# Linear attention ahead of a Mish feed-forward on one core: the side of each attention product that stands still on TensorE, how x is divided and turned, and where the key units run

## The chip, the cores and the metric

The program runs on one NeuronCore of a Trainium2 chip. The metric is the device time of one execution in microseconds (us), and for the kernel before it is the median of three runs. A run can also leave a profile, and its span is the time from the first to the last recorded instruction.

## What is computed

There are 8 batches, 8 heads, 576 tokens, head width 64 and 128 features. With x for q or k:

```python
proj = x @ w_phi                                  # 64 -> 128
proj = proj - max(abs(proj), axis=-1)
phi  = concat([exp(proj), exp(-proj)], axis=-1)   # 256 features
kv   = sum over tokens of phi(k)[f] * v[d]        # 256 x 64 for each batch and head
z    = sum over tokens of phi(k)[f]
x    = (phi(q) @ kv) / (phi(q) @ z + 1e-6)        # 4608 tokens x 512 after the heads are joined
h    = x @ w_in                                   # 512 -> 2048
out  = (h * tanh(softplus(h))) @ w_out            # 2048 -> 512 (this h*tanh(softplus) is Mish)
```

The weights of the feed-forward arrive as float64 words and are turned to float32 on the core.

## The kernel before, in words

**Number forms.** A float32 product is done in one of two ways. In plain float32 each matmul of the program becomes two instructions of TensorE. Or an operand is split into a high and a low part in the type float32r, and three products (high by high, high by low, low by high) are added up; each is one instruction. The feed-forward uses three products throughout.

**Feed-forward.** The 4608 tokens are 18 chunks of 256. For each chunk, 16 steps `ff_in` (L364) make h, twelve matmuls of 256 columns each; `mish` applies Mish on ScalarE two steps at a time and splits the result into `gh` and `gl`; 16 steps `ff_out` (L395) add up the output, six matmuls of 512 columns each. They follow each other with a lag of some four steps.

**Attention, keys.** A key unit is 256 tokens of a head pair (or the end of one pair and the beginning of the next): `k_load`, `k_proj` and `k_sum`. There are 72, nine to a batch. `project` (L161) multiplies keys by `w_phi` in six matmuls of 256 columns into `pp_k`; VectorE takes the largest absolute value (`m_k`, L146) and subtracts it (`d_k`, L165); ScalarE makes both exponentials. In `k_sum` (L223) the sums over tokens have **v as the stationary operand** (66 columns: 64 of v, one of ones for z, one of zeros) and both exponentials moving, 256 columns, in plain float32, into `kvps`. The result lies the wrong way round, so it is copied (`kvT`), turned by four transposes (`kvt`, L230), copied again, and written to DRAM, from which `kv_load` reads it back when queries need it.

**Attention, queries.** A query unit is one of four head pairs `cc` of a chunk `c`. `project_stacked` (L177) makes `pp_q` with four matmuls of 256 columns; `q_turn` (L262) turns the result by four transposes into `dt_q`; `q_exp` makes both exponentials and splits each into `eh` and `el`; `q_kv` splits `kv` into `kvs`. `q_num` (L313) has **kv as the stationary operand** (66 columns) and the exponentials moving: twelve matmuls where the chunk lies in one batch, 24 shorter ones where it touches two. Its result is already transposed for `ff_in`. The denominators are one row of it, so `q_den` sends them through DMA onto many partitions (`dp`), takes the reciprocal, writes it to DRAM (`r`) and spreads it back (`rb`); `q_out` multiplies on GpSimd and splits x into `xTh` and `xTl`. The first chunk's projection and sums are done in plain float32.

**What sets the order.** A list of events with due times, in units of one feed-forward step, gives the program order: all 72 key units and the first chunk's four query units come 1.1 units apart before step 0, the weight pieces (32 of 512 KB, each loaded and then converted by VectorE, ScalarE and GpSimd) are spread evenly over the same time, and the query units of chunk c+1 run at a pitch of four steps among the feed-forward of chunk c. A scheduler then orders each engine's queue; each engine works its queue strictly in order. All DMAs are issued by the SP queue. PSUM has four buffers `att` for all attention results, two for h and two for the output; before step 0, `project` uses the two of h and `kvps` the two of the output.

Of the kernel before, what the change touches and what calls it, by code (L numbers as in the profile page):

```python
# [27 lines left out]
NRAW, NE, NEH, NEL, NV, NKV = 3, 4, 2, 2, 2, 5  # L28
NHALF, NX, NRB, NXT, NG = 2, 2, 1, 3, 4

GP, GQ, GV = 2.2, 2.2, 1.5
GK, VLOAD = 2.7, 1.5
LOAD, WLOAD, KVLOAD = 4.0, 3.0, 3.0
Q0, Q1, QOUT, QL = -1.0, 4.0, 4.5, 0.5
QPOS, UPRE = 60, 1.1
W0, W1 = 4.0, 2.0
LAG, TAIL, TAILLAG = 4, 10, 2

KPLAIN, QPLAIN = 1, 1

NSPARE, WIN, MSPARE = 32, 4, 5
# [3 lines left out]
def attention_then_mish(ctx, tc, qT, kT, va, w_phi, w_in, w_out, out):  # L45
# [5 lines left out]
    dram = ctx.enter_context(tc.tile_pool(name="dram", bufs=4, space=bass.MemoryType.DRAM))  # L51
# [13 lines left out]
    def raw_tile(name):  # L65
        return work.tile([P, 2, 2 * P], F32, tag="raw", name=name, bufs=NRAW)

    def half_tile(name):
        return work.tile([P, 512], F32, tag="half", name=name, bufs=NHALF)


    wphi_raw = moe.tile([P, 2 * F], F32, tag="xTh", name="wphi_raw", bufs=NXT)
    nc.sync.dma_start(wphi_raw, w_phi[0])
    wphi_hi = moe.tile([P, 2 * F], F32R, tag="gh", name="wphi_hi", bufs=NG)
    wphi_lo = moe.tile([P, 2 * F], F32R, tag="gl", name="wphi_lo", bufs=NG)
    nc.vector.tensor_copy(wphi_hi, wphi_raw)
    nc.vector.tensor_sub(wphi_lo, wphi_raw, wphi_hi.bitcast(F32))
    wst_raw = moe.tile([P, 2 * F], F32, tag="xTl", name="wst_raw", bufs=NXT)
    nc.sync.dma_start(wst_raw, w_phi[1])
# [10 lines left out]
    spare = [f"w{kind}_{i}_{j}" for kind, i, j in pieces[-NSPARE:]]  # L90
    turn = 0
# [5 lines left out]
    def pair_tile(name):  # L97
        nonlocal turn
        if len(spare) >= MSPARE:
            turn += 1  # L100
            return slot_tile(spare[turn % min(WIN, len(spare))], F32, name)
        return work.tile([P, 2, 512], F32, tag="e", name=name, bufs=NE)

    piece = 0

    def load_weight(kind, i, j):
        nm = f"{kind}_{i}_{j}"
        if f"w{nm}" in spare:
            spare.remove(f"w{nm}")
        src = w_in[i * P:(i + 1) * P, j * 512:(j + 1) * 512] if kind == "in" else w_out[i * P:(i + 1) * P, :]  # L110
        slot = f"w{kind}_{i}_{j}"
        words = slot_tile(slot, U32, f"words_{nm}").rearrange("p a b -> p (a b)")
        nc.sync.dma_start(words, src.bitcast(U32))
        weight[kind, i, j] = words.rearrange("p (a b) -> p a b", b=2)

    def split_weight(kind, i, j):

        nonlocal piece
        nm = f"{kind}_{i}_{j}"
        slot = f"w{kind}_{i}_{j}"  # L120
        words = weight[kind, i, j]
        low, high = words[:, :, 0], words[:, :, 1]
        tag, bufs = ("u", 3) if piece % 5 < 3 else ("ee", 2)
        piece += 1
        w = moe.tile([P, 512], U32, tag=tag, name=f"w_{nm}", bufs=bufs)
# [10 lines left out]
        parts = slot_tile(slot, F32R, slot)  # L136
# [5 lines left out]
    def less_max(d, name):  # L142

        d3 = d.rearrange("p (n f) -> p n f", f=F)
        m = work.tile([P, 4], F32, tag="m", name=f"m_{name}", bufs=3)
        nc.vector.tensor_reduce(m, d3, axis=AX.X, op=ALU.max, apply_absolute_value=True)  # L146
        return d3, m.unsqueeze(2).broadcast_to([P, 4, F])

    def project(raw, plain, name):

        parts = ((raw, wphi_raw),)
        if not plain:
            hl = work.tile([P, 2, 2 * P], F32R, tag="hl", name=f"hl_{name}")
            hi, lo = hl[:, 0, :], hl[:, 1, :]
            nc.scalar.copy(hi, raw)  # L155
            nc.gpsimd.tensor_sub(lo, raw, hi.bitcast(F32))  # L156
            parts = ((hi, wphi_hi), (hi, wphi_lo), (lo, wphi_hi))
        ps = (ps_h if starting else ps_att).tile([P, 512], F32, tag="h" if starting else "att", name=f"pp_{name}")
        for i in range(2):
            for k, (x, w) in enumerate(parts):  # L160
                nc.tensor.matmul(ps[:, i * 2 * F:(i + 1) * 2 * F], x[:, i * P:(i + 1) * P], w,  # L161
                                 start=(k == 0), stop=(k == len(parts) - 1))
        d = pair_tile(f"d_{name}")
        p3, m = less_max(ps, name)
        nc.vector.tensor_tensor(d[:, 0, :].rearrange("p (n f) -> p n f", f=F), p3, m, op=ALU.subtract)  # L165
        return d

    def project_stacked(raw, name):

        x = work.tile([P, 2, 2 * P], F32R, tag="hl", name=f"hl_{name}")  # L170
        nc.scalar.copy(x, raw)  # L171
        nc.gpsimd.tensor_sub(x[D:], raw[D:], x[D:].bitcast(F32))  # L172
        d = pair_tile(f"d_{name}")
        for i in range(2):
            ps = ps_att.tile([P, 2, 2, F], F32, tag="att", name=f"pp{i}_{name}")
            for j in range(2):
                nc.tensor.matmul(ps[:, j], x[:, j, i * P:(i + 1) * P], wst, start=True, stop=True)  # L177
            di = d[:, 0, i * 2 * F:(i + 1) * 2 * F].rearrange("p (j f) -> p j f", f=F)
            nc.scalar.copy(di, ps[:, :, 1, :])
            nc.vector.tensor_tensor(di, ps[:, :, 0, :], di, op=ALU.add)  # L180
# [101 lines left out]
    def batches(c):  # L282
        return range(c * CH // S, (c * CH + CH - 1) // S + 1)
# [213 lines left out]
```

## Time and profile before

| what | value |
|---|---|
| median of three runs | 1228.69 us (1226.5 to 1229.23) |
| the profiled execution | 1229.93 us |
| its span | 1228.0 us |
| mean granted TensorE clock | 0.996 |
| busy in the span: PE / PEld / DVE / ACT / POOL | 1199.2 / 1064.4 / 597.2 / 895.2 / 594.9 us |
| instructions of PE and of PEld | 8094 each |

PE is TensorE's matrix products, PEld its loads of the stationary operand, DVE VectorE, ACT ScalarE, POOL GpSimd, SPq the queue that issues DMAs. A load can run while the product ahead of it streams, so PE and PEld overlap. The end of a matmul is modelled, so the time of one is best read from the distance between starts. In a group "128*66 128x256" the stationary operand has 128 partitions and 66 columns, and 256 columns move. A float32 matmul shows as two instructions.

### The profile page before, as it was taken

Reading aid. Unit: us, or ns where it says so; the run is one execution under the profiler, and the core shown is the slowest. Engines: PE = TensorE matmul, PEld = TensorE weight load, DVE = VectorE, ACT = ScalarE, POOL = GpSimd, SP = SyncE. Lnnn points to the kernel's source line nnn. Section 1 sums busy time; section 2 is a strip of 40 time slices with the busy share of each in tenths; the row PEclk is TensorE's granted clock in tenths of the full one; section 3 lists DMA queues with packets and bytes.
Section 4 is the critical chain, followed back from the end, with each engine's and each line's share of the span. In section 5 each row is a group of like instructions: output and inputs, shape, how many; then the busy total and the mean of one; then the engine's idle time right before and its main releaser. Section 6 shows DMA issues by size and latency. Waiting matters only on the chain.

```text
span 1228.0 us, 21711 instructions
## 1 busy us (share of the span) xinstructions
PE 1199.2 (98%) x8094; PEld 1064.4 (87%) x8094; DVE 597.2 (49%) x987; ACT 895.2 (73%) x1704; POOL 594.9 (48%) x509
## 2 busy tenths in 40 slices
PE   8999998899999999999999999999999999999998
PEld 6776776688999899999999999999999999999997
DVE  6987887954443344334443444334343444344211
ACT  6887877788777767777777777777777777777531
POOL 3765665856544545454444544545454544544200
PEclk9999999899999999999999999999999999999999
DMA  5665657311111211110121111111111111010000
GB/s 194 206 187 176 200 159 229 99 57 36 53 44 40 61 31 51 38 53 27 49 65 36 44 28 56 31 53 27 57 61 32 44 40 53 27 36 14 25 24 18
DMA packets 62025, 84.87 MB, mean 69 GB/s; under 512 B 17632, under 2 KB 35808, under 8 KB 61920
## 3 DMA queue, kind: packets, MB, share of 16 engines
q1 hardware_dynamic: 61920, 83.49, 22.0%
q8 instruction: 63, 1.03, 0.3%
q14 instruction: 42, 0.34, 0.1%
HBM read 69.40 MB, written 13.91 MB: 68 GB/s over the span
## 4 chain that ended last, share of the span: by engine, by line
PE 81%; DVE 7%; DMA 5%; ACT 2%; issue 2%; POOL 1%; SPq 0%; POOLq 0%; DVEq 0%
PE h L364 33%; PE o L395 32%; PE num_q L313 8%; PE kvps L223 3%; PE pp_q L177 2%; PE dt_q L262 2%; DMA words_out<-w_out 2%; DMA words_in<-w_in 2%; DVE m_k L146 1%; DVE d_k L165 1%; PE pp_k L161 1%; DVE scale_in L133 1%; DVE scale_out L128 1%; DMA rb<-r 1%; DVE w_in L132 1%
## 5 line engine op out<-in xcount | busy, mean ns | idle before, releaser
L364 PE MATMUL h<-xTh,win 128*128 128x256 f32 x2304 | 466.3, 284 | 0.0
L381 DVE TENSOR_TENSOR gl<-u,gh 128x256 fp32r<-128x256 f32 x288 | 169.1, 613 | 479.6 <-ACT gh L380 476.5
L364 PEld LDWEIGHTS h<-xTh,win 128*128 128x128 f32 x2304 | 378.2, 190 | 9.4
L395 PE MATMUL o<-wout,gh 128*128 128x512 f32 x1152 | 364.5, 396 | 0.0
L364 PE MATMUL h<-xTl,win 128*128 128x256 f32 x1152 | 325.3, 283 | 0.0
L279 POOL TENSOR_TENSOR el_q<-d_q,eh_q 128x512 fp32r<-128x512 f32 x136 | 180.0, 1335 | 295.4 <-ACT eh_q L278 295.4
L364 PEld LDWEIGHTS h<-xTl,win 128*128 128x128 f32 x1152 | 219.0, 190 | 6.8
L395 PE MATMUL o<-wout,gl 128*128 128x512 f32 x576 | 224.8, 391 | 0.0
L395 PEld LDWEIGHTS o<-wout,gh 128*128 128x128 f32 x1152 | 198.4, 189 | 25.8
L223 PE MATMUL kvps<-d_k,v 128*66 128x256 f32 x640 | 151.9, 383 | 5.4 <-ACT d_k L207 4.4
L172 POOL TENSOR_TENSOR hl_q<-qraw,hl_q 64x512 fp32r<-64x512 f32 x68 | 88.5, 1301 | 105.5 <-ACT hl_q L171 90.2
L272 ACT ACTIVATE d_q<-dt_q 128x512 f32<-128x512 f32 x144 | 86.1, 601 | 71.6 <-PE dt_q L262 71.3
L395 PEld LDWEIGHTS o<-wout,gl 128*128 128x128 f32 x576 | 108.3, 188 | 23.8
L223 PEld LDWEIGHTS kvps<-d_k,v 128*66 128x66 f32 x640 | 86.0, 139 | 48.2 <-ACT d_k L207 6.7
L380 ACT CAST gh<-u 128x256 fp32r<-128x256 f32 x288 | 109.0, 406 | 20.5 <-PE o L395 11.9
L372 ACT ACTIVATE u<-h 128x512 f32<-128x512 f32 x144 | 86.1, 598 | 49.7 <-PE h L364 49.0
L313 PE MATMUL num_q<-eh_q,kvs 128*66 128x256 f32 (+3 forms) x736 | 107.9, 255 | 0.9 <-ACT eh_q L278 0.9
L298 POOL TENSOR_TENSOR kvs<-kv,kvs 128x264 fp32r<-128x264 f32 x92 | 81.4, 895 | 19.3 <-ACT kvs L297 13.7
L313 PE MATMUL num_q<-el_q,kvs 128*66 128x256 f32 (+3 forms) x368 | 88.9, 256 | 1.2 <-POOL el_q L279 1.2
L372 ACT ACT_TABLE_LOAD x69 | 88.5, 1283 | 1.2
L156 POOL TENSOR_TENSOR hl_k<-kraw,hl_k 128x256 fp32r<-128x256 f32 x71 | 60.5, 856 | 57.8 <-ACT hl_k L155 57.7
L161 PE MATMUL pp_k<-wphi_hi,hl_k 128*128 128x256 f32 x284 | 76.3, 331 | 10.9 <-DVE d_k L165 9.8
(74 smaller groups left out, 1694.9 us busy)
## 6 DMA issues: line engine op xcount, KB each, us to landing
qraw<-qT SPq DMA_DIRECT2D x136, 128.0 KB, 3.0
v<-va SPq DMA_DIRECT2D x32, 330.0 KB, 3.4
kraw<-kT SPq DMA_DIRECT2D x36, 256.0 KB, 3.5
rb<-r SPq DMA_DIRECT2D x72, 128.0 KB, 3.0
out<-osb SPq DMA_DIRECT2D x36, 256.0 KB, 2.1
words_in<-w_in SPq DMA_DIRECT2D x16, 512.0 KB, 4.4
words_out<-w_out SPq DMA_DIRECT2D x16, 512.0 KB, 4.1
kvd<-kvo SPq DMA_DIRECT2D x32, 132.0 KB, 1.8
```

The costliest lines, as they stand in the source:

```text
L161: nc.tensor.matmul(ps[:, i * 2 * F:(i + 1) * 2 * F], x[:, i * P:(i + 1) * P], w, start=(k == 0), stop=(k == len(parts) - 1))
L172: nc.gpsimd.tensor_sub(x[D:], raw[D:], x[D:].bitcast(F32))
L223: nc.tensor.matmul(kv_ps[pair][:VW, j], vt[:, slot, j, :], e[:, :, (2 * i + j) * F:(2 * i + j + 1) * F], start=(slot == 0 and j == 0), sto ...
L272: nc.scalar.activation(e, ps, AF.Exp, scale=2.0 * s - 1.0)
L279: nc.gpsimd.tensor_sub(el, e, eh.bitcast(F32))
L298: nc.gpsimd.tensor_sub(wl, w, wh.bitcast(F32))
L313: nc.tensor.matmul(ps[:VW, j, r0:r1], w[:, j, s, :], e[:, j * CH + r0:j * CH + r1], start=first, stop=(s == 1 and k == len(parts) - 1), sk ...
L364: nc.tensor.matmul(ps, w[:, wcol], x[:, cc % 2, :], start=(n == 0), stop=(n == 11))
L372: nc.scalar.activation(u, hv, AF.Mish)
L380: nc.scalar.copy(gh, u[:, f * CH:(f + 1) * CH])
L381: nc.vector.tensor_sub(gl, u[:, f * CH:(f + 1) * CH], gh.bitcast(F32))
L395: nc.tensor.matmul(ps, g[:, cols], w, start=(i == 0 and k == 0), stop=(i == NFT - 1 and k == 2))
```

## The change

Every product of the attention now has the activations standing still and a narrow operand moving. `project` (one for keys and queries) loads the same 64 rows twice, splits the second copy, and does eight matmuls of 128 columns, x stationary. In `k_sum` the exponentials are stationary (128 columns) and v moves (66 columns), in plain float32; the sum comes out as it is needed, so the copy, the transposes and the way through DRAM go, and `kv` stays in the core's memory. In `q_num` the exponentials are stationary and `kv` moves, 66 columns in plain float32, eight matmuls, or more where a tile of tokens touches two batches; the splits of the exponentials and of `kv` go. The result has tokens on partitions, so the denominators are a column: two small operations and one product on VectorE divide it, and the DMAs of `q_den` go. `q_out` then turns x by four transposes and splits it on ScalarE and VectorE.

Only 16 key units come before step 0 now, with the first chunk's queries between them; the other 56 run among the feed-forward, one in four steps. The weight pieces are spread up to step 9. A chain of order among ScalarE's exponentials and Mish (`table`) is written out.

```diff
-NRAW, NE, NEH, NEL, NV, NKV = 3, 4, 2, 2, 2, 5
-NHALF, NX, NRB, NXT, NG = 2, 2, 1, 3, 4
+NRAW, NHL, NE, NV, NKV = 4, 3, 4, 3, 9
+NHALF, NX, NXT, NG = 2, 3, 3, 4
...
+GP, GQ, GX = 2.2, 2.2, 0.8
+GK, GE, VLOAD = 4.4, 1.3, 3.0
+Q0, Q1, K0 = -1.0, 4.0, 2.0
+KFIRST, UPRE, KPITCH = 16, 1.1, 4.0
+W0, W1 = 2.0, 9.0
...
+    def table(act):
+        nonlocal last
+        if last is not None:
+            tc.add_manual_dep(act.ins, last.name, mybir.DependencyInfo(mybir.DependencyClass.NoSync, mybir.DependencyReason.DATA),
+                              reason="table")
+        last = act.ins
...
-    def project(raw, plain, name):
...
+    def project(raw, name):
+        x = work.tile([P, 512], F32R, tag="hl", name=f"hl_{name}", bufs=NHL)
+        nc.scalar.copy(x, raw)
+        nc.gpsimd.tensor_sub(x[D:], raw[D:], x[D:].bitcast(F32))
+        ps = (ps_h if starting else ps_att).tile([P, 4, F], F32, tag="h" if starting else "att", name=f"pp_{name}")
+        for n in range(4):
+            for k in range(2):
+                nc.tensor.matmul(ps[:, n], x[:, n * P:(n + 1) * P], wst[:, k * F:(k + 1) * F], start=(k == 0), stop=(k == 1))
+        e = work.tile([P, 2, 512], F32, tag="e", name=f"e_{name}", bufs=NE)
+        m = work.tile([P, 4], F32, tag="m", name=f"m_{name}", bufs=3)
+        nc.vector.tensor_reduce(m, ps, axis=AX.X, op=ALU.max, apply_absolute_value=True)
+        nc.vector.tensor_tensor(e[:, 0, :].rearrange("p (n f) -> p n f", f=F), ps,
+                                m.unsqueeze(2).broadcast_to([P, 4, F]), op=ALU.subtract)
+        return e
...
     def k_sum(b, u):
...
                 for j in range(2):
-                    nc.tensor.matmul(kv_ps[pair][:VW, j], vt[:, slot, j, :], e[:, :, (2 * i + j) * F:(2 * i + j + 1) * F],
-                                     start=(slot == 0 and j == 0), stop=(slot == 4), skip_group_check=True)
+                    for s in range(2):
+                        n = 2 * j + i
+                        nc.tensor.matmul(ps[:, j, s], e[:, s, n * P:(n + 1) * P], vt[:, slot, j, :],
+                                         start=(slot == j == s == 0), stop=(slot == 4), skip_group_check=True)
                 if slot == 4:
-                    kvT = half_tile(f"kvT_{b}_{pair}")
...
+                    kv[b, pair] = work.tile([P, 2, 2, VW], F32, tag="kv", name=f"kv_{b}_{pair}", bufs=NKV)
+                    nc.vector.tensor_copy(kv[b, pair], kv_ps.pop(pair))
...
     def q_num(c, cc):
-        nm = f"q_{c}_{cc}"
...
+        e = q_live.pop((c, cc))
+        ps = ps_att.tile([P, 2, 2, VW], F32, tag="att", name=f"num_{c}_{cc}")
+        for t in range(2):
+            b, r = divmod((2 * c + t) * P, S)
+            rows = ((b, 0, P),) if r + P <= S else ((b, 0, S - r), (b + 1, S - r, P))
+            for j in range(2):
+                n = 2 * j + t
+                for b, r0, r1 in rows:
+                    for s in range(2):
+                        nc.tensor.matmul(ps[r0:r1, t, j], e[:, s, n * P + r0:n * P + r1], kv[b, cc][:, j, s],
+                                         start=(s == 0), stop=(s == 1), skip_group_check=True)
...
+        nc.vector.tensor_scalar(r, ps[:, :, :, D], 1e-6, None, op0=ALU.add)
+        nc.vector.reciprocal(r, r)
+        nc.vector.tensor_tensor(x, ps[:, :, :, :D], r.unsqueeze(3).broadcast_to([P, 2, 2, D]), op=ALU.mult)
...
-    def q_den(c, g):
...
     def q_out(c, g):
...
+        x = x_live.pop((c, g))
+        ps = ps_att.tile([P, 2, CH], F32, tag="att", name=f"xt_{c}_{g}")
         for i in range(2):
+            for t in range(2):
+                nc.tensor.transpose(ps[:, i, t * P:(t + 1) * P], x[:, i, t], ident)
...
-        nc.gpsimd.tensor_mul(x, x, rb)
-        nc.scalar.copy(hi, x)
-        nc.gpsimd.tensor_sub(lo, x, hi.bitcast(F32))
+        nc.scalar.copy(hi, ps)
+        nc.vector.tensor_sub(lo, ps, hi.bitcast(F32))
...
-    seq = [("k", b, u) for b in range(B) for u in range(9)]
-    seq[QPOS:QPOS] = [("q", 0, cc) for cc in range(NCC)]
...
+    first = [("k", n) for n in range(9)]
+    rest = [("k", n) for n in range(9, KFIRST)]
+    for cc in range(NCC):
+        first.append(("q", cc))
+        if cc < len(rest):
+            first.append(rest[cc])
+    first += rest[NCC:]
...
+    for n in range(KFIRST, 9 * B):
+        k_unit(K0 + (n - KFIRST) * KPITCH, n)
...
```

**TensorE among the feed-forward, before.** Around the query units 1 and 2 of chunk 9, ahead of the feed-forward step h_8_2 (`eh`, `el` and `kvs` are the split parts):

```order
L364 MATMUL h_8_2_8047<-xTh_8_1_7969,win_3_0_475 128x256
L177 MATMUL pp0_q_9_2_8064<-wst_93,hl_q_9_2_8060 128x256 x2
L177 MATMUL pp1_q_9_2_8069<-wst_93,hl_q_9_2_8060 128x256 x2
L313 MATMUL num_q_9_1_8080<-eh0_q_9_1_8007,kvs_9_1_4_8038 66x256 x2
L313 MATMUL num_q_9_1_8080<-el0_q_9_1_8008,kvs_9_1_4_8038 66x256
L313 MATMUL num_q_9_1_8080<-eh0_q_9_1_8007,kvs_9_1_4_8038 66x256 x2
L313 MATMUL num_q_9_1_8080<-el0_q_9_1_8008,kvs_9_1_4_8038 66x256
L313 MATMUL num_q_9_1_8080<-eh1_q_9_1_8012,kvs_9_1_4_8038 66x256 x2
```

**The same place now.**

```order
L281 MATMUL o_7_1_6332<-wout_13_0_1597,gl1_7_6_6699 128x512
L132 MATMUL pp_k_5_4_6881<-wst_85,hl_k_5_4_6878 128x128 x8
L177 MATMUL kvps_5_1_6733<-v_5_1_6554,e_k_5_3_6720 128x66 x8
L254 MATMUL h_8_2_6907<-xTh_8_0_6309,win_0_0_233 128x256
L254 MATMUL h_8_2_6907<-xTl_8_0_6310,win_0_0_233 128x256
```

and eleven instructions on

```order
L254 MATMUL h_8_2_6907<-xTl_8_1_6649,win_3_0_369 128x256
L254 MATMUL h_8_2_6907<-xTh_8_1_6648,win_3_0_369 128x256
L132 MATMUL pp_q_9_2_6923<-wst_85,hl_q_9_2_6920 128x128 x8
L217 MATMUL num_9_1_6939<-kv_4_1_5523,e_q_9_1_6773 128x66 x8
L254 MATMUL h_8_2_6907<-xTh_8_0_6309,win_0_0_233 128x256
L254 MATMUL h_8_2_6907<-xTl_8_0_6310,win_0_0_233 128x256
```

A key unit (`pp_k`, `kvps`) stands among the feed-forward, the projection of a query unit is eight matmuls of 128 columns instead of four of 256, and `num` is eight matmuls of 66 columns, each of them two instructions, with `e_q` standing still.

**TensorE ahead of the first `ff_in`, before.** Where the sums of batch 1 begin:

```order
L223 MATMUL kvps_0_3_353<-d_k_0_8_330,v_0_3_214 66x256 x4
L161 MATMUL pp_k_1_2_428<-wphi_hi_87,hl_k_1_2_425 128x256
L161 MATMUL pp_k_1_2_428<-wphi_lo_88,hl_k_1_2_425 128x256
L161 MATMUL pp_k_1_2_428<-wphi_hi_87,hl_k_1_2_425 128x256 x2
L161 MATMUL pp_k_1_2_428<-wphi_lo_88,hl_k_1_2_425 128x256
L161 MATMUL pp_k_1_2_428<-wphi_hi_87,hl_k_1_2_425 128x256
L223 MATMUL kvps_1_0_441<-d_k_1_0_366,v_1_0_318 66x256 x4
L161 MATMUL pp_k_1_3_453<-wphi_hi_87,hl_k_1_3_450 128x256
L161 MATMUL pp_k_1_3_453<-wphi_lo_88,hl_k_1_3_450 128x256
L161 MATMUL pp_k_1_3_453<-wphi_hi_87,hl_k_1_3_450 128x256 x2
```

**Now.**

```order
L198 MATMUL dt_0_1_620<-ident_74,e_q_0_1_556 128x128 x4
L217 MATMUL num_0_0_627<-kv_0_0_283,e_q_0_0_442 128x66 x8
L132 MATMUL pp_q_0_2_646<-wst_85,hl_q_0_2_643 128x128 x8
L177 MATMUL kvps_1_0_694<-v_1_0_508,e_k_1_0_504 128x66 x8
L177 MATMUL kvps_1_0_694<-v_1_0_508,e_k_1_1_599 128x66 x7
L198 MATMUL dt_0_2_723<-ident_74,e_q_0_2_655 128x128 x3
L132 MATMUL pp_k_1_2_681<-wst_85,hl_k_1_2_678 128x128 x8
L198 MATMUL dt_0_2_723<-ident_74,e_q_0_2_655 128x128
L217 MATMUL num_0_1_732<-kv_0_1_378,e_q_0_1_556 128x66 x8
L132 MATMUL pp_q_0_3_748<-wst_85,hl_q_0_3_745 128x128 x8
```

The first chunk's queries (`pp_q`, `dt`, `num`) now stand around the first sums of batch 1, and the sums of this batch wait for `v_1_0`, with `dt_0_2`, `num_0_1` and `pp_q_0_3` of the first chunk queued behind them.

**The SP queue at the load of `v_1_0`, before.**

```order
L113 DMA words_in_3_0_376<-w_in 128x1024
L113 DMA words_in_1_0_216<-w_in 128x1024
L234 DMA kvd_0_0_207<-kvo_0_0_205 128x264
L200 DMA v_0_3_214<-va 128x660
L193 DMA kraw_7_408<-kT 128x512
L234 DMA kvd_0_1_279<-kvo_0_1_277 128x264
L200 DMA v_1_0_318<-va 128x660
L113 DMA words_in_2_0_300<-w_in 128x1024
L193 DMA kraw_8_478<-kT 128x512
```

**Now.** The last weight pieces and what follows them:

```order
L82 DMA words_in_1_3_1193<-w_in 128x1024
L82 DMA words_in_2_3_1238<-w_in 128x1024
L121 DMA qraw_0_2_458<-qT 64x512 x2
L82 DMA words_in_3_3_1292<-w_in 128x1024
L82 DMA words_out_12_0_1360<-w_out 128x1024
L82 DMA words_out_13_0_1396<-w_out 128x1024
L82 DMA words_out_14_0_1449<-w_out 128x1024
L82 DMA words_out_15_0_1500<-w_out 128x1024
L152 DMA v_1_0_508<-va 128x660
L121 DMA kraw_1_2_510<-kT 64x512 x2
L121 DMA qraw_0_3_560<-qT 64x512 x2
L121 DMA kraw_1_3_605<-kT 64x512 x2
```

All 32 weight pieces are now ahead of `v_1_0`, where four were.

More of the change, by code (lines that the diff above doesn't have):

```diff
@@ L140, in split_weight @@
         nc.gpsimd.tensor_sub(lo, w, hi.bitcast(F32))
[L142 to L147, printed above, removed]
-    def project(raw, plain, name):
[L151 to L166, printed above, removed]
```

266 lines of the change are left out of this document (66 added, 200 removed).

## The prediction

> **What bounds the kernel now.** I read the page's head first, then busy time by stage, then TensorE's rows in order of time, since the answer to the first two is TensorE.
>
> ```profile
> span 1228.0 us, 21711 instructions
> PE 1199.2 (98%) x8094; PEld 1064.4 (87%) x8094; DVE 597.2 (49%) x987; ACT 895.2 (73%) x1704; POOL 594.9 (48%) x509
> ```
>
> ```profile
> 0.00:240.00 240.00, 217.28 (x1247) 162.29 (x1248) 197.56 (x322) 184.71 (x359) 149.71 (x144) 0.99 0.59 184
> 240.00:1190.00 950.00, 947.94 (x6645) 871.98 (x6645) 394.34 (x654) 702.57 (x1329) 445.18 (x366) 1.00 0.14 42
> ```
>
> In the second fence the columns are the stage, its length, the busy time of PE, PEld, VectorE, ScalarE and GpSimd, the granted clock, the DMA share and GB/s. From 240 to 1190 us TensorE has no free time, so whatever leaves ScalarE, VectorE, GpSimd or the DMAs there is worth nothing by itself, and every microsecond of TensorE work counts in full. Before 240 TensorE is still the busiest, with VectorE at 198 of 240 behind it. Each matmul has its own load (8094 and 8094), also where two in a row use the same stationary operand. So the sum is a sum over TensorE instructions, plus the time in which it has nothing to do.
>
> Prices come from distances between starts. From the timeline of TensorE:
>
> ```profile
> 112.01 0.41 PE L230 MATMUL kvt<-ident,kvT 66*128 66x66 f32 x4
> 112.25 1.89 PE L223 MATMUL kvps<-d_k,v 128*66 128x256 f32 x8
> ...
> 704.71 0.63 PE L177 MATMUL pp_q<-wst,hl_q 128*128 128x256 f32 x4
> 705.18 0.40 PE L313 MATMUL num_q<-eh_q,kvs 128*66 128x256 f32 x2
> ...
> 706.59 0.28 PE L364 MATMUL h<-xTh,win 128*128 128x256 f32 x1
> ...
> 712.24 0.60 PE L262 MATMUL dt_q<-ident,d_q 128*128 128x128 f32 x4
> 712.59 0.36 PE L364 MATMUL h<-xTh,win 128*128 128x256 f32 x1
> 712.79 0.28 PE L364 MATMUL h<-xTl,win 128*128 128x256 f32 x1
> ```
>
> and from the chain that ended last:
>
> ```profile
> 11.55 3.45 PE kvps L223 x16
> ...
> 289.64 1.43 PE h L364 x12
> 292.94 1.79 PE num_q L313 x24
> ...
> 308.81 2.75 PE o L395 x12
> ...
> 416.55 1.46 PE num_q L313 x24
> ```
>
> A 256-column float32r product takes 1.43/12 = 0.119 us, a 512-column one 2.75/12 = 0.229, one of the two instructions of a 256-column float32 product 3.45/16 = 0.2156, `pp_q` 0.47/4 = 0.1175, four `kvt` 0.24, four `dt` with the switch behind them 712.79 - 0.12 - 712.24 = 0.43, and twelve `num` of 256 columns 706.59 - 705.18 = 1.41.
>
> The work before, with counts from the program: h 3456 x 0.119 = 411; o 1728 x 0.229 = 396; `pp_k` 426 x 0.119 = 51; `pp_q` 272 x 0.1175 = 32 and 20 plain instructions 4; `kvps` 640 x 0.2156 = 138; `kvt` 32 x 0.24 = 8; `dt` 72 x 0.43 = 31; `num` 44 x 1.41 + 16 x 1.79 + 8 x 1.46 + 32 plain x 0.2156 = 109. That is 1180 of 1228; 204 of it stands ahead of the first h in TensorE's queue. The next rows say when that is:
>
> ```profile
> 237.72 0.36 PE L161 MATMUL pp_k<-wphi_hi,hl_k 128*128 128x256 f32 x1 [2.25 <-DVE d_k L165]
> ...
> 238.51 0.28 PE L364 MATMUL h<-xTh,win 128*128 128x256 f32 x1
> ```
>
> So TensorE lacks 238.5 - 204 = 34.5 us ahead of the first h, and 989.5 - 976 = 13 behind it. The first number will change, the second I keep.
>
> **The change: the price of a load.** The new `pp`, `kvps` and `num` have 128 columns standing still and 128 (float32r) or 66 (float32) moving: 1152 + 1280 + 1024 = 3456 instructions at one unknown price r, and 256 at the tiles that touch two batches. Streaming alone is cheap: 66/256 x 0.2156 = 0.056 for an instruction of `kvps`, 128/256 x 0.119 = 0.060 for `pp`, 0.0575 on the mean. That is the lower end. The upper end is 0.119, the h product, which has such a load under it. No row has a load of 128 columns under a shorter float32 stream, so the load has to be worked out:
>
> ```profile
> 513.75 0.25 PE L313 MATMUL num_q<-eh_q,kvs 128*66 128x64 f32 x2
> ...
> 514.08 0.37 PE L313 MATMUL num_q<-eh_q,kvs 128*66 128x192 f32 x2
> ```
>
> ```profile
> L364 PEld LDWEIGHTS h<-xTh,win 128*128 128x128 f32 x2304 | 378.2, 190 | 9.4
> L223 PEld LDWEIGHTS kvps<-d_k,v 128*66 128x66 f32 x640 | 86.0, 139 | 48.2 <-ACT d_k L207 6.7 <-DMA v<-va 1.2 <-issue 1.1
> L313 PEld LDWEIGHTS num_q<-eh_q,kvs 128*66 128x66 f32 x736 | 83.7, 137 | 1.6 <-ACT eh_q L278 1.2
> L230 PEld LDWEIGHTS kvt<-ident,kvT 66*128 66x128 f32 x128 | 11.9, 141 | 2.3 <-ACT kvT L227 1.2
> ```
>
> Six products of 64 columns take 0.33 us, 0.055 each, though 64/256 of 0.119 is 0.030: there the load of 66 columns sets the pace. A load of 128 columns lasts 190 ns and one of 66 lasts 137, so 62 columns cost 0.053 us more; 0.055 + 0.053 gives **r = 0.108**. The one row against it is `kvt`, a load of 128 columns every 0.060; but its load lasts only 141, so a transpose loads in another way, and I don't take its price.
>
> Now the work after: h and o 807; `pp` 1152 x 0.108 = 124; `kvps` 1280 x 0.108 = 138; `num` 1024 x 0.108 + 256 x 0.055 (loads of 64 columns or fewer) = 125; `dt` 31; the new `xt` 36 x 0.43 = 15. Sum 1240, **60 more**. Nearly all of it is the query side: a unit's projection and `num` were 0.47 + 1.41 and become 0.86 + 1.73. The key sums come out even, 138 and 138: half the stream, but twice the loads, each longer.
>
> **The change: the start.** Ahead of the first h TensorE now has 63 us: 544 of the 3456 instructions, 59, and transposes, 4. What else stands there? VectorE works its queue in order, and ahead of the `xTl` that the first h needs it has about 24 weight pieces and 21 units' maximum and subtraction.
>
> ```profile
> 0.00:240.00 240.00, 19.20 (x31) 0.99 0.59 184
> ...
> 0.00:240.00 240.00, 20.94 (x32) 0.99 0.59 184
> ...
> 0.00:240.00 240.00, 24.77 (x31) 0.99 0.59 184
> ...
> 0.00:240.00 240.00, 28.92 (x31) 0.99 0.59 184
> ```
>
> ```profile
> L146 DVE TENSOR_REDUCE m_k<-pp_k 128x4 f32<-128x512 f32 x72 | 49.0, 681 | 10.3 <-PE pp_k L161 10.2
> L165 DVE TENSOR_TENSOR d_k<-pp_k,m_k 128x512 f32<-128x512 f32 x72 | 49.1, 684 | 1.1
> ...
> L232 DVE COPY kvo<-kvt 128x264 f32<-128x264 f32 x32 | 13.5, 422 | 2.1 <-PE kvt L230 2.1
> ```
>
> ```profile
> 7.49 0.69 DVE L146 TENSOR_REDUCE m_k<-pp_k 128x4 f32<-128x512 f32 x1 [3.37 <-PE pp_k L161]
> ```
>
> The first four rows are VectorE in the first 240 us for lines 127, 128, 132 and 133 alone, the next three groups by line (busy time, then mean ns of one), the last the first use of VectorE for a key unit; 0.62 + 0.65 + 0.80 + 0.93 = 3.0 us a piece. So 24 x 3.0 + 21 x 1.365 + 5 copies x 0.42, and some 5 for dividing and splitting x (estimated from the copy and the subtraction of like size), make 108; begun at 7.5, without a gap, 115. At the 0.82 of before it would be 7.5 + 132 = 139. I take 121, nearer the tight end, since it is now VectorE that the others wait for.
>
> The SP queue could be later: the load `v_1_0`, which the sums of batch 1 and, behind them in TensorE's queue, the rest of the first chunk's queries wait for, now stands behind all 32 weight pieces.
>
> ```profile
> words_in<-w_in SPq DMA_DIRECT2D x16, 512.0 KB, 4.4
> v<-va SPq DMA_DIRECT2D x32, 330.0 KB, 3.4
> ```
>
> With 14 key and query loads of 256 KB (two halves each) that is some 22 MB. At the stage's 184 GB/s it takes 118 us, at its rate per busy share (184/0.59 = 312) 70. VectorE, with 20 pieces and 14 units done, reaches this place at some 93 and has 25 us left behind it, so the first h could slip to 143; this is the upper end of the start. With h at 121, TensorE lacks 58 ahead of it, **24 more** than before.
>
> What costs nothing: the removed DMAs of denominators and kv, the splits on GpSimd and the copies on ScalarE were under a TensorE busy 947.94 of 950. What is added there is covered too: 56 key units put 56 x 1.365 = 76 us on VectorE, busy 394 of 950, and ScalarE, at 703, loses the second exponentials and gains the keys':
>
> ```profile
> L278 ACT ACTIVATE eh_q<-dt_q 128x512 fp32r<-128x512 f32 x136 | 82.3, 605 | 0.0
> L206 ACT ACTIVATE d_k<-d_k 128x512 f32<-128x512 f32 x72 | 45.1, 628 | 14.2 <-DVE d_k L165 14.2
> ```
>
> (56 units x 2 x 0.628 = 70.) If that cover fails it is the last rival below. The first h waits for x, and x for a reciprocal instead of six DMAs; both happen inside the 121.
>
> Sum: 1228 + 60 + 24 = 1312 as a span. The profiled execution is 1.9 over its span and the median of the runs 1.2 under that execution, so **1312 us**. Per unit of r, 2912 of the 3456 instructions stand behind the first h: the time is 1312 + 2912 (r - 0.108), and breaks even at r = 0.079.
>
> **The rivals.** *The stream sets the pace, and the change wins.* If loads of 128 columns hide under streams of 66 as in `kvt`, r is 0.0575 and the time 1312 - 147 = 1165. For it: `kvt` at 0.060. Against it: the 64-column products at twice their stream, and 190 against 137. It decides below r = 0.079.
>
> *Loads hide in part.* `dt` has 128 columns standing and 128 moving and takes 0.35/4 = 0.0875; with this r the time is 1252. Its loads are transposes' too, which speaks against it. The Trainium skill, on its page "TensorE: Matmul & The Clock Gate", section "Back-to-back issue gap", gives about 81 ns for sustained pairs of load and product at 128 columns; by it the time would be 1233. That section also gives 131 ns at 512 columns, where this trace has 229, so I give it little.
>
> *New waits among the feed-forward.* One or two of the four `att` buffers are now held by `kvps` over many steps, and a projection that finds none free stops TensorE, with h and o queued behind it. The row at 237.72 shows such a wait, 2.25 us. If the 56 key units there wait 1 us each, 1312 + 56 = 1368. Against it: eight matmuls and more stand between a projection and what follows from it.
>
> **How the numbers follow.** The load sets the pace: 0.78; the stream does: 0.12; in part: 0.04; new waits: 0.06. The likeliest by itself reaches from r = 0.104 and a start at 115 (1312 - 12 - 6 = 1294) to r = 0.119 and a start at 143 (1312 + 32 + 22 = 1366). The range 1258 to 1368 holds it and what lies near it; the streaming case and half of the waits are left out. About 0.2% is what a measurement of this kernel can tell from no change. Faster is the streaming case and a little of the partial one, 0.13; the same 0.02; slower 0.85.
>
> **What would show it.** In the profile after: `pp`, `kvps` and `num` starting every 0.105 to 0.12 us, with loads of 190 ns; PE busy all through the feed-forward, a chunk with key units near 69 us (807/18 = 44.8, four query units of 3.2, four key units of 2.8); the first h between 115 and 143 us, VectorE over 90% busy ahead of it; `kvps` near 138 us in all. Starts 0.06 apart would make the forecast wrong at once; a first h after 150, or idle time of TensorE between 300 and 1200, would mean that the start or the waits were mis-sized.

## The result and the profile after

The changed kernel takes **1372.31 us** (median of four runs, 1371.79 to 1373.19), the kernel before beside it 1228.64: a ratio of 1.1174, 95% interval 1.1154 to 1.1193. It is slower by 144 us where 83 were forecast, 4 us above the upper end of the range. The sign and the price of the new products were right; the start, the time up to the first product of the feed-forward ("the first h"), was not. Where a run of a kernel lies over 1.5% above the fastest one, the others alone are compared with the kernel before.

The span of the changed kernel, then its windows (length; busy time and instructions of PE, PEld, VectorE, ScalarE, GpSimd; granted clock; DMA share; GB/s):

```profile
span 1370.3 us, 22755 instructions
```

```profile
80.00:100.00 20.00, 10.78 (x50) 10.39 (x50) 20.00 (x27) 11.84 (x21) 12.58 (x10) 1.00 0.05 13
...
140.00:160.00 20.00, 20.00 (x96) 20.00 (x96) 6.54 (x12) 6.66 (x12) 4.07 (x4) 1.00 0.27 77
...
0.00:165.00 165.00, 125.85 (x580) 123.65 (x580) 132.91 (x172) 86.09 (x144) 101.07 (x78) 1.00 0.54 170
...
300.00:1200.00 900.00, 900.00 (x6660) 843.37 (x6658) 288.98 (x613) 468.12 (x768) 127.07 (x100) 1.00 0.15 45
```

Three things stand here. From 300 to 1200 us TensorE has no free time at all. Between 80 and 100 us VectorE has none (20.00 of 20), and TensorE half its time. And from 140 to 160 TensorE is busy for all 20 us with only 96 instructions, 0.208 us each, though the clock column reads 1.00. TensorE's timeline shows the same by distances between starts:

```profile
6.49 7.22 PE L132 MATMUL pp_k<-wst,hl_k 128*128 128x128 f32 x32 [6.49 <-POOL hl_k L128]
...
151.50 1.95 PE L132 MATMUL pp_q<-wst,hl_q 128*128 128x128 f32 x8
153.24 3.62 PE L177 MATMUL kvps<-v,e_k 128*128 128x66 f32 x16
156.66 3.62 PE L217 MATMUL num<-kv,e_q 128*128 128x66 f32 x16
...
165.15 0.56 PE L254 MATMUL h<-xTh,win 128*128 128x256 f32 x1
...
170.14 0.28 PE L254 MATMUL h<-xTl,win 128*128 128x256 f32 x1
...
701.92 1.00 PE L132 MATMUL pp_q<-wst,hl_q 128*128 128x128 f32 x8
702.76 1.95 PE L217 MATMUL num<-kv,e_q 128*128 128x66 f32 x16
704.52 0.37 PE L254 MATMUL h<-xTh,win 128*128 128x256 f32 x1
...
714.80 2.84 PE L177 MATMUL kvps<-v,e_k 128*128 128x66 f32 x24
717.45 0.37 PE L254 MATMUL h<-xTh,win 128*128 128x256 f32 x1
```

At 702 to 717 eight `pp` take 0.84 us (0.105 each), sixteen `num` 1.76 (0.110), 24 `kvps` 2.65 (0.110). Before 165 the same eight `pp` take 1.74 (0.2175) and sixteen `kvps` 3.42 (0.214): **half speed**, from the first product on and until 170. The kernel before begins at half speed too, but leaves it after 5.5 us; in its timeline the starts, 0.21 apart, come closer at 10.9:

```profile
5.41 2.05 PE L161 MATMUL pp_k<-wphi_raw,kraw 128*128 128x256 f32 x4 [5.41 <-DMA kraw<-kT]
...
10.04 0.41 PE L161 MATMUL pp_k<-wphi_lo,hl_k 128*128 128x256 f32 x1
10.26 0.67 PE L161 MATMUL pp_k<-wphi_hi,hl_k 128*128 128x256 f32 x2
...
11.15 0.28 PE L161 MATMUL pp_k<-wphi_lo,hl_k 128*128 128x256 f32 x1
11.27 0.28 PE L161 MATMUL pp_k<-wphi_hi,hl_k 128*128 128x256 f32 x1
```

The first h starts at 165.15, not at 121. Of these 165 us TensorE is busy 125.85, twice the 63 that the work takes at full speed. For most of the rest it waits for VectorE (waits of TensorE in the first 165 us: total, times, longest):

```profile
PE dt L198 <- DVE e_q L136: 15.7, 4, 6.2
PE pp_k L132 <- DVE e_k L136: 12.3, 5, 6.3
PE pp_k L132 <- POOL hl_k L128: 6.5, 1, 6.5
```

What VectorE does there shows between 81 and 86 us, in its timeline and, below, in GpSimd's:

```profile
81.00 0.41 DVE L93 TENSOR_SCALAR scale_out<-words_out 128x512 uint32<-128x512 uint32 x1
81.33 1.75 DVE L97 SCALAR_TENSOR_TENSOR w_out<-words_out,w_out 128x512 f32<-128x512 uint32 x1
83.01 1.48 DVE L93 TENSOR_SCALAR scale_out<-words_out 128x512 uint32<-128x512 uint32 x1
84.41 0.68 DVE L135 TENSOR_REDUCE m_q<-pp_q 128x4 f32<-128x512 f32 x1
```

```profile
81.22 1.32 POOL L100 TENSOR_TENSOR w_out<-w_out,scale_out 128x512 f32<-128x512 f32 x1 [1.97 <-DVE w_out L97]
82.50 3.11 POOL L105 TENSOR_TENSOR wout<-w_out,wout 128x512 fp32r<-128x512 f32 x2
```

The operation of line 93 takes 0.41 us while GpSimd waits, and 1.48 while GpSimd subtracts; the reduction of a result in PSUM (L135) takes 0.68 beside the next subtraction, what it takes elsewhere. The Trainium skill, on its page "SBUF — State Buffer", section "Who interferes with whom", says that VectorE and GpSimd share a port pair as a lock: whichever comes second stands for the whole of the other's instruction, and a VectorE operation without a second SBUF operand or a two-port mode isn't touched. The rows agree.

### The profile page after: what moved, and what is told of

It is laid out like the page before. It is cut to its first block, busy times and chain, and to the rows that moved or that the text cites. A ratio compares the mean times of both kernels' runs of the same rounds, so it can differ in the third digit from the quotient of the medians.

```text
span 1370.3 us, 22755 instructions
## 1 busy us (share of the span) xinstructions
PE 1324.4 (97%) x9328; PEld 1243.1 (91%) x9328; DVE 532.1 (39%) x993; ACT 704.3 (51%) x1165; POOL 277.4 (20%) x214
## 4 chain that ended last, share of the span: by engine, by line
PE 89%; DVE 7%; issue 1%; ACT 1%; SPq 1%; DMA 0%; ACTq 0%; DVEq 0%
PE h L254 30%; PE o L281 29%; PE num L217 9%; PE kvps L177 9%; PE pp_q L132 4%; PE pp_k L132 4%; PE dt L198 2%; PE xt L232 1%; DVE scale_out L98 1%; DVE w_in L97 1%; DVE w_in L92 1%; DVE scale_in L93 1%; DVE w_out L92 1%; DVE scale_in L98 1%; DVE w_out L97 1%
## 5 line engine op out<-in xcount | busy, mean ns | idle before, releaser
L267 DVE TENSOR_TENSOR gl<-u,gh 128x256 fp32r<-128x256 f32 x288 | 123.1, 444 | 496.5 <-ACT gh L266 488.6
L177 PE MATMUL kvps<-v,e_k 128*128 128x66 f32 x1280 | 185.1, 308 | 3.7 <-ACT e_k L161 3.7
L177 PEld LDWEIGHTS kvps<-v,e_k 128*128 128x128 f32 x1280 | 179.1, 224 | 4.3 <-ACT e_k L161 4.2
L127 ACT CAST hl_k<-kraw 128x512 fp32r<-128x512 f32 x72 | 44.3, 615 | 247.6 <-PE pp_q L132 217.6
L217 PE MATMUL num<-kv,e_q 128*128 128x66 f32 (+1 forms) x1280 | 145.7, 275 | 0.0
L217 PEld LDWEIGHTS num<-kv,e_q 128*128 128x128 f32 (+1 forms) x1280 | 138.7, 190 | 2.0
L128 POOL TENSOR_TENSOR hl_k<-kraw,hl_k 64x512 fp32r<-64x512 f32 x72 | 92.9, 1290 | 223.2 <-ACT hl_k L127 219.2
L135 DVE TENSOR_REDUCE m_q<-pp_q 128x4 f32<-128x512 f32 x72 | 49.7, 690 | 223.8 <-PE pp_q L132 223.8
L132 PEld LDWEIGHTS pp_k<-wst,hl_k 128*128 128x128 f32 x576 | 87.9, 224 | 24.2 <-issue 13.2
L132 PE MATMUL pp_k<-wst,hl_k 128*128 128x128 f32 x576 | 87.7, 304 | 18.8 <-DVE e_k L136 12.3
```

Source lines behind the costliest of these rows:

```text
L132: nc.tensor.matmul(ps[:, n], x[:, n * P:(n + 1) * P], wst[:, k * F:(k + 1) * F], start=(k == 0), stop=(k == 1))
L135: nc.vector.tensor_reduce(m, ps, axis=AX.X, op=ALU.max, apply_absolute_value=True)
L177: nc.tensor.matmul(ps[:, j, s], e[:, s, n * P:(n + 1) * P], vt[:, slot, j, :], start=(slot == j == s == 0), stop=(slot == 4), skip_group_c ...
L217: nc.tensor.matmul(ps[r0:r1, t, j], e[:, s, n * P + r0:n * P + r1], kv[b, cc][:, j, s], start=(s == 0), stop=(s == 1), skip_group_check=True)
L267: nc.vector.tensor_sub(gl, u[:, f * CH:(f + 1) * CH], gh.bitcast(F32))
```

## The experiments

My theory after the result: the arithmetic costs what was forecast, and the start has two causes laid on one another, VectorE slowed beside GpSimd and TensorE at half speed under narrow streams. The rivals: one of them alone, the order of the units, or the longer loads. All medians stand beside a median of before of 1228.64 to 1230.93.

### Denser work ahead of each projection

```diff
+        if starting:
+            for _ in range(8):
+                nc.tensor.matmul(ps.rearrange("p n f -> p (n f)"), x[:, :P], x, start=True, stop=True)
```

> The changed kernel with eight extra 512-column products ahead of each projection until the first ff_in (22 units; their result is overwritten by the projection, so the output stays). Theory A (TensorE runs at half speed until the first dense products of the feed-forward, because loads of 128 columns under short streams leave the array idle half of the time, and this holds the first h back): the pairs in the start go from one in 0.215 us to one in 0.11, the stretch of 37 us between the end of VectorE's load and the first h shrinks by some 15 us although work is added, the first h comes near 145 to 152 and the time is 1352 to 1360. Rival B (VectorE alone sets the start, TensorE's half speed is hidden under it): first h not before 165, time 1372 or, with the added products at half speed (22 x 3.7 = 80 us, in part under idle time), up to 1410.

Measured: 1364.34 us (1363.84 to 1365.85), first h at 158.9. TensorE now runs at full speed for much of the start (eight `pp` in 0.84 us, the extra products 0.24 each), so what stands in its queue does decide its speed. But 23 units with eight products of 0.24 are 44 us of added work, and VectorE is as late as before: 131.1 us busy of the first 158. The net gain is 8 us, less than theory A had expected (1352 to 1360, first h at 145 to 152).

### The weights without GpSimd

```diff
-        nc.gpsimd.tensor_tensor(w, w, scale.bitcast(F32), op=ALU.mult)
...
-        nc.gpsimd.tensor_sub(lo, w, hi.bitcast(F32))
+        nc.scalar.copy(lo, scale.bitcast(F32))
```

> The changed kernel without GpSimd in the conversion of the weights: the product of mantissa and scale is left out and the low part is a copy on ScalarE, so the weights are wrong; all else stays. Theory C (VectorE's weight operations last 4.2 us a piece in the start instead of 3.0 because GpSimd works beside them): a piece falls to 2.2 to 2.4 us of VectorE, VectorE is through its part ahead of the first h some 45 us earlier, and the first h then waits for TensorE alone, at 0.215 us a pair 126 us of work: first h near 140, time near 1345. Rival (the DMAs or VectorE's own queue made them slow): pieces stay over 4 us, first h at 165, time 1372.

Measured: **1336.82 us** (1333.75 to 1338.69), first h at 136.3. VectorE's groups of the first 130 us (busy time, mean ns of one), of the changed kernel and then of this one:

```profile
L97 DVE SCALAR_TENSOR_TENSOR w_out<-words_out,w_out 128x512 f32<-128x512 uint32 x11 | 12.5, 1135 | 0.2 <-ACT w_out L95 0.2
L92 DVE TENSOR_SCALAR w_out<-words_out 128x512 uint32<-128x512 uint32 x11 | 11.7, 1072 | 0.0
```

```profile
L97 DVE SCALAR_TENSOR_TENSOR w_out<-words_out,w_out 128x512 f32<-128x512 uint32 x11 | 9.7, 879 | 0.1
L92 DVE TENSOR_SCALAR w_out<-words_out 128x512 uint32<-128x512 uint32 x11 | 5.2, 477 | 1.8 <-DMA words_out<-w_out 1.3 <-ACT wout L103 0.3 <-ACT win L103 0.2
```

VectorE's instructions are the same, and shorter: its four operations on a piece take 2.6 us here and 4.3 in the changed kernel (2.2 to 2.4 were expected). It is busy 7.5 of the 20 us from 100 on. What holds the first h now is TensorE at half speed (a window of this kernel):

```profile
100.00:120.00 20.00, 20.00 (x97) 20.00 (x97) 7.50 (x16) 7.18 (x14) 5.06 (x4) 1.00 0.19 57
```

So GpSimd's part in the weights costs 35 us, and the other cause is what is left.

### The order alone

```diff
-W0, W1 = 4.0, 2.0
+W0, W1 = 2.0, 9.0
+KFIRST, K0, KPITCH = 16, 2.0, 4.0
...
+    keys = [("k", b, u) for b in range(B) for u in range(9)]
+    seq, rest = keys[:9], keys[9:KFIRST]
...
+    for i, (kind, a, j) in enumerate(keys[KFIRST:]):
+        k_unit(K0 + KPITCH * i, a, j)
```

This is the kernel before, with its own arithmetic, in the new order (some buffers got their own names for it).

> The kernel before with the order part alone: 16 key units and the first chunk's queries ahead of step 0, the other 56 key units one in four steps, weight pieces up to step 9; its arithmetic (v and kv stationary) stays. Three small buffers get their own names and one pool has three buffers instead of four so that it fits. If the start alone costs: TensorE's work stays 1180, the first h comes near 130 with 60 us of work done, so 1130 + 130 + 13 = 1270 (1250 to 1290). If the order is harmless and only the arithmetic costs: 1228. With dense 256-column products TensorE should be at full speed in the start (0.12 and 0.2156 us).

Measured: **1291.15 us** (1290.69 to 1291.21), 61.5 more than before and 1 us above the range expected. Windows and TensorE's waits of this kernel:

```profile
100.00:120.00 20.00, 4.99 (x16) 3.61 (x17) 19.90 (x26) 11.97 (x22) 13.49 (x11) 0.50 0.19 60
...
0.00:130.00 130.00, 75.09 (x357) 52.10 (x357) 105.02 (x148) 80.42 (x150) 85.28 (x71) 0.83 0.56 186
130.00:300.00 170.00, 152.05 (x1002) 132.59 (x1001) 114.25 (x154) 123.69 (x236) 103.99 (x84) 0.95 0.20 60
```

```profile
PE dt_q L263 <- DVE d_q L183: 18.9, 3, 14.6
PE pp_k L162 <- DVE d_k L166: 12.5, 6, 5.8
PE kvps L224 <- DMA v<-va: 12.0, 1, 12.0
```

TensorE lacks 55 us ahead of the first h (at 130) and 18 in the 170 us behind it, where the kernel before lacks 23 ahead of its first h by the same busy time. The order has a cost of its own: the conversion of the weights must be done while only 16 key units' worth of TensorE work is there to cover it. That TensorE would run at full speed here, with 256 columns moving, did not hold throughout: its clock is 0.83 over the first 130 us, and 0.50 from 100 to 120, behind a wait of 14.6 us for VectorE. So a part of the 62 is half speed too; how much isn't worked out.

### 128 columns of v moving

```diff
-                        nc.tensor.matmul(ps[:, j, s], e[:, s, n * P:(n + 1) * P], vt[:, slot, j, :],
+                        nc.tensor.matmul(ps[:, j, s], e[:, s, n * P:(n + 1) * P], vt[:, slot].rearrange("p j w -> p (j w)")[:, 4 * j:4 * j + P],
```

> The changed kernel with 128 columns moving in the key sums instead of 66 (both heads' v; the wanted 66 are copied out), the same loads. Theory D (the load of 128 columns sets the pace): 1280 instructions stay near 0.110 to 0.120 us, time within +15 us of 1372. Rival (the stream has a part in the price): each of them 0.05 us longer, +55 to +65 us.

Measured: **1346.74 us** (1344.59 to 1349.25): nearly twice the stream, and 26 us *less*. Neither side had expected a gain. Among the feed-forward sixteen `kvps` take 1.76 us, 0.110 each as with 66 columns:

```profile
500.29 2.00 PE L177 MATMUL kvps<-v,e_k 128*128 128x128 f32 x16
502.05 0.37 PE L256 MATMUL h<-xTh,win 128*128 128x256 f32 x1
```

So the stream hides under the load there, as the price of the prediction has it. The gain is in the start: the first h comes at 141.2 instead of 165.2. Timeline of this kernel:

```profile
13.56 3.74 PE L177 MATMUL kvps<-v,e_k 128*128 128x128 f32 x18
17.06 1.09 PE L132 MATMUL pp_k<-wst,hl_k 128*128 128x128 f32 x8
17.99 1.78 PE L177 MATMUL kvps<-v,e_k 128*128 128x128 f32 x14
...
28.66 1.94 PE L132 MATMUL pp_k<-wst,hl_k 128*128 128x128 f32 x8 [5.33 <-DVE e_k L136]
```

After some 4 us of `kvps` with 128 columns moving TensorE reaches full speed (eight `pp` in 0.93 us, from 17.06 to 17.99). After a wait of 5.33 us it is at half speed again. In the changed kernel, with 66 columns, it stays at half through a stretch without any gap that ends with the first h.

### Both at once

The edits of "The weights without GpSimd" and of "128 columns of v moving" together, to see if the two causes add up. As in the first of them, a part of the weights' conversion is left out.

> The changed kernel with two of the earlier edits at once: the low part of the weights is copied on ScalarE without GpSimd's product and subtraction (part of the weights' conversion is left out), and 128 columns instead of 66 move in the key sums. Theory (two causes lay on one another in the start: VectorE was slowed beside GpSimd, and TensorE ran at half speed under narrow streams): with both gone TensorE's 63 us of work at full speed and VectorE's 62 us of conversion no longer hold the first h to 130 or later; first h at 95 to 115, span 1290 to 1315. Rival (one cause alone explains it, and what the other edit gained was the same time): no better than the better of the two alone, first h at 130 or later, 1325 to 1340. Second rival (128 columns help by something behind the first h): the gain shows after the first h, not ahead of it.

Measured: **1309.44 us** (1308.95 to 1313.25), 63 less than the changed kernel; one alone gave 35, the other 26. The first h, in its timeline:

```profile
103.67 0.36 PE L255 MATMUL h<-xTh,win 128*128 128x256 f32 x1
```

Behind it stand 1307.1 - 103.7 = 1203 us, in the changed kernel 1370.3 - 165.2 = 1205: all but 2 us of the gain lie ahead of the first h. The two gains add up (35 + 26 = 61), so the theory of two causes holds, and both rivals fall.

### The key sums alone, turned

```diff
-                    nc.tensor.matmul(kv_ps[pair][:VW, j], vt[:, slot, j, :], e[:, :, (2 * i + j) * F:(2 * i + j + 1) * F],
-                                     start=(slot == 0 and j == 0), stop=(slot == 4), skip_group_check=True)
+                    for s in range(2):
+                        n = 2 * i + j
+                        nc.tensor.matmul(ps[:, j, s], e[:, s, n * P:(n + 1) * P], vt[:, slot, j, :],
+                                         start=(slot == j == s == 0), stop=(slot == 4), skip_group_check=True)
...
-                    nc.scalar.copy(kvT[:VW], kv_ps.pop(pair)[:VW].rearrange("w j s f -> w (j s f)"))
```

> The kernel before with the key sums alone turned (phi stands, v moves in float32, the result is copied once; no copy to SBUF and transposes back); queries, their division and the order stay as before. By the load price of the prediction (0.108 us an instruction of 66 columns): key sums 138 us as before, the transposes' 8 us gone, so 1220 (1212 to 1235), with all key units still ahead of or early in the program. Rival (TensorE drops to half its speed under narrow streams in the start): the 1000 or more such instructions ahead of the first h take 0.21 us instead of 0.108, first h at 280 or later instead of 238, 1270 to 1340.

Measured: 1248.47 us (1247.05 to 1257.33), ratio 1.0161 (1.0119 to 1.0204), first h at 252.5: between the two. The timeline shows why:

```profile
120.00 0.36 PE L161 MATMUL pp_k<-wphi_hi,hl_k 128*128 128x256 f32 x1 [1.47 <-DVE d_k L165]
...
120.79 7.58 PE L225 MATMUL kvps<-v,d_k 128*128 128x66 f32 x40
128.12 0.56 PE L161 MATMUL pp_k<-wphi_hi,hl_k 128*128 128x256 f32 x1
```

Ahead of these rows TensorE is at full speed, and the projections still move 256 columns. A wait of 1.47 us comes, and in the long run of `kvps` behind it TensorE falls to half speed (forty take 7.33 us, 0.18 each); the projection behind them runs at half speed too. Such stretches stand at 120, 160 and 220 us:

```profile
120.00:140.00 20.00, 20.00 (x135) 20.00 (x135) 12.97 (x23) 12.34 (x24) 10.54 (x11) 0.74 0.51 148
...
220.00:240.00 20.00, 19.15 (x86) 18.38 (x86) 18.57 (x25) 12.94 (x23) 17.98 (x15) 0.50 0.37 109
```

Here the clock column shows them (0.50 to 0.74). In the changed kernel it reads 1.00, perhaps since it had not changed yet.

### The same with 128 columns moving

The edit to the moving operand shown above, on this kernel.

> The kernel before with the key sums alone turned, as in the earlier run of that part, and 128 columns of v moving instead of 66 (the surplus is not copied on). Theory (that run's 19 us came from stretches of half speed ahead of the first h, at 120, 160 and 220 us, which a denser stream removes): first h at 238 to 246, no stretch at half speed ahead of it, 1222 to 1238. Rival (the 19 us are the longer loads' own price, 0.108 to 0.115 an instruction, with waits behind them): first h at 250 or later, 1245 to 1260, since each instruction is then a little longer and nothing shorter.

Measured: 1239.31 us (1237.13 to 1240.68), ratio 1.0067 (1.0051 to 1.0083), first h at 241.5, clock 1.00 in every window to 200 us and 0.91, 0.92 and 0.82 in the next three. It is 9 us faster with twice the stream, the stretches of half speed mostly gone; 1 us above the theory's range and below the rival's. With most of the loss of speed gone, turned key sums still save no time: some 8 us more than before, to which the stretches that are left may add.

### The query side alone

```diff
+            for k in range(2):
+                nc.tensor.matmul(ps[:, n], x[:, n * P:(n + 1) * P], wst[:, k * F:(k + 1) * F], start=(k == 0), stop=(k == 1))
...
+                        nc.tensor.matmul(ps[r0:r1, t, j], e[:, s, n * P + r0:n * P + r1], kv[b, cc][:, j, s],
+                                         start=(s == 0), stop=(s == 1), skip_group_check=True)
...
+                nc.tensor.transpose(ps[:, i, t * P:(t + 1) * P], x[:, i, t], ident)
```

> The kernel before with the query side alone changed (weights move over 128 standing columns in the projection, phi stands in the numerators, x is divided by row and transposed on TensorE); key sums, their order and the DMAs of keys and weights stay as before. Theory (the load price: pp 0.108 instead of 0.229 per 512 columns, num 1.73 instead of 1.41 a unit): TensorE's sum behind the first h rises by 60, so 1288 (1270 to 1300), with no change ahead of the first h. Rival (the query side costs less than the sum because loads overlap in the mixed program): under 1255. Rival (half speed in the start comes from the query units there): first h later than 245, over 1300.

Measured: **1283.51 us** (1281.85 to 1286.38), 54 more than before, first h at 241.4 instead of 238.5. One window shows that TensorE has no free time behind the first h, so its sum sets the time:

```profile
240.00:1270.00 1030.00, 1029.93 (x7342) 948.17 (x7341) 291.23 (x662) 528.16 (x840) 87.03 (x69) 1.00 0.10 30
```

ScalarE, VectorE and GpSimd have less to do than before (291, 528 and 87 us for VectorE, ScalarE and GpSimd, where the kernel before has 398, 709 and 445 from 240 to 1220), and it brings nothing. The theory holds.

### The changed arithmetic in the order of before

The turned key sums and the changed query side together; the keys' projection and the way of kv through DRAM stay as before.

> The kernel before with the key sums turned and the query side changed, both as in the changed kernel, but with the order of before: all 72 key units ahead of the first h, the weights' conversion spread over them (the keys' projection and the way of kv over memory stay as before too). Theory (the change's parts add up: keys +19, queries +54, the order and its bunched conversion of weights the rest of 144): 1228 + 74 = 1302 (1292 to 1315), first h at 250 to 260. Rival (the changed arithmetic makes the start slow whatever the order, since nearly all streams ahead of the first h are now narrow): first h at 300 or later, 1345 or more.

Measured: two of the four runs took 1293.22 and 1300.36 us, a ratio of 1.0537 (1.0504 to 1.0571). That is 66 more than before where the parts give 19 + 54 = 73, and it lies in the theory's range. The other two took 1319.29 and 1342.75, so the four lie 50 us apart, where those of the kernel before lie within 5. The execution of 1319.29 is the profiled one; one of its windows:

```profile
180.00:200.00 20.00, 20.00 (x96) 20.00 (x95) 10.59 (x18) 8.63 (x16) 6.55 (x6) 0.50 0.46 129
```

Behind a wait of 1.47 us that ends at 161 TensorE is at half speed, and it comes back only at 223, after 60 us of work with hardly a gap. The first h of this execution comes at 284.5, 25 us later than expected. No other run of this kernel has a profile, so that they differ by the length of such stretches is likely and not shown.

## Why the prediction was wrong, point by point

**The price of a load: right.** I gave 0.108 us for each of the new instructions; at full speed they take 0.105 (`pp`) and 0.110 (`num`, `kvps`). Loads, not streams, set the pace: 128 columns moving cost 0.110 as well as 66. The streaming rival and the partly hidden loads are out. The Trainium skill's page "TensorE: Matmul & The Clock Gate", section "Back-to-back issue gap", gives about 0.081 at 128 columns. These rows don't agree with it.

**The work after, +60: right.** The query side, nearly all of it, measures 54 by itself. Behind the first h the changed kernel has 1205 us where the forecast had 1190: a chunk with key units takes 70.0 us where I had near 69, for fourteen chunks some 15 us. Between these two rows of the chain of waits lie four chunks:

```profile
238.45 2.03 PE h L254 x17
...
518.59 2.03 PE h L254 x17
```

Part of it stands at the change from a float32 product to h, 0.20 us from 704.52 to the next start instead of 0.119; the rest I can't assign to a row.

**What costs nothing, and new waits: right.** TensorE is busy 900.00 of 900 from 300 to 1200. Its waits behind the first h come to 2.6 us, one of 2.2 for a copy of `kv` among them; the rival had 56.

**The start: wrong.** This is the step that failed, in two of its terms. *"0.62 + 0.65 + 0.80 + 0.93 = 3.0 us a piece"* was a mean over a stage in which pieces lie 7.5 us apart. Packed closer, one every 4.7 us from 16 to 127, and beside GpSimd's own part of the same pieces, the four operations take 100 us for 23.5 pieces, **4.3 each**: 30 us more for 24 pieces. *"TensorE now has 63 us"* priced the start at the speed of the feed-forward. It took **126**, at half speed. The kernel before has such rows, and I hadn't weighed them: its first 5.5 us, and a second stretch behind a wait of 2.57 us, in a window (200 to 230 us) with a clock of 0.89:

```profile
218.23 0.55 PE L161 MATMUL pp_k<-wphi_hi,hl_k 128*128 128x256 f32 x1 [2.57 <-DVE d_k L165]
218.58 0.41 PE L161 MATMUL pp_k<-wphi_lo,hl_k 128*128 128x256 f32 x1
218.79 0.63 PE L161 MATMUL pp_k<-wphi_hi,hl_k 128*128 128x256 f32 x2
```

The starts lie 0.21 apart here, and 0.12 again from 225 on. So the first h came at 165 instead of 121, 44 us of the 60 by which I missed; the 15 behind it make the rest. With both causes taken away the first h came at 104 and the time was 1309, beside a forecast of 1312. That these two meet is luck: the first h is 17 us earlier there than forecast, with only 2.7 us of VectorE for a piece, and the work behind it 12 us longer.

**The upper end of 143 for the start** was put on the SP queue and `v_1_0`. It wasn't that: from 80 to 100 us the DMAs are at a share of 0.05 while VectorE is full. The bound had the wrong cause, and so was no bound. In the old arithmetic under the same order a wait of 12.0 us for a load of v does stand.

**The signs in the profile** that I had named were the right ones: a first h after 150 was to mean that the start was mis-sized.

By parts, measured alone: key sums 19, queries 54, order 62, together 135 of 144. The order, +24 in the forecast, is the largest; it was forecast as a wait for VectorE at a price per piece that was too low, and that is a part of it: 31 us of TensorE's waits in the run of the order alone are for VectorE, beside the 12.0 for v and the half speed. No run changes the keys' projection alone; at the prediction's price it adds 62 - 51 = 11, near the 9 that the parts leave over.

What stays open: what measure of TensorE's activity decides its speed (stream width matters, as the runs with 128 columns show, but they don't say if it counts columns, rows or time), and how the 62 of the order would divide among conversion, the load of v and half speed in the old arithmetic.

## What to carry to other kernels

Price a product by its load when the moving side is narrower than the standing one, and price it again wherever TensorE is not kept dense: here a stretch of narrow streams ran at half speed for as long as it lasted, 160 us. A mean duration is valid for the spacing it was taken at; when work is packed closer, look at the longest durations of the group and at what runs beside them (in the first 130 us of the kernel before, line 132 had a median of 683 ns and a longest of 1142 for `w_in`). And moving work behind the first product of the main stage takes away the cover of everything that must still come ahead of it.

## What the runs showed of the hardware

- TensorE stays at half speed (0.214 us an instruction instead of 0.110) through 37 us of work without a gap, from 128 to 165, under streams of 66 and 128 columns with loads of 128. The Trainium skill, page "TensorE: Matmul & The Clock Gate", section "What's actually happening", has it return to full speed after about 3.4 us of sustained work. The kernel before comes near that (5.5 us, with a wait of 0.32 in them); the changed one doesn't.
- A wider stream under the same loads made a program faster, by 26 us in the changed kernel and 9 in the one with turned keys. The product itself takes no longer at full speed: 0.110 us with 66 columns and with 128.
- The clock column can read 1.00 at half speed: distances between starts are the surer reading.
- VectorE's operations on SBUF take up to 1.75 us instead of 0.68, and 1.48 instead of 0.41, beside a product or a subtraction on GpSimd; a reduction from PSUM takes the same 0.68 beside one.
